# Edge values copied by products on GpSimd, and the filter's maxima begun twelve turns later, in a kernel of a spectral filter and a feed-forward block

## The chip, the cores and the metric

The kernel runs on one core of a Trainium2 chip. The metric is device time in microseconds (us) of one execution; the number given for a kernel is the median of its runs. The engines of the core are called by short names: PE (TensorE, matrix products), DVE (VectorE, elementwise work and reductions), ACT (ScalarE, activations and copies with a scale), POOL (GpSimd), SP (SyncE, which here only issues DMAs). Each works through its own list of instructions in order; semaphores make one wait for another.

## The reference

```python
def _layernorm(x, axis=-1, eps=1e-5):
    m = jnp.mean(x, axis=axis, keepdims=True)
    v = jnp.var(x, axis=axis, keepdims=True)
    return (x - m) / jnp.sqrt(v + eps)

xn = _layernorm(A_x)                         # (1, 2048, 1024)
X = jnp.fft.rfft2(xn, axes=(-2, -1))
s = jnp.fft.irfft2(X * (A_w_r + 1j * A_w_i), (2048, 1024), axes=(-2, -1))
h = _silu(jnp.einsum("bsd,df->bsf", xn, B_w1))      # w1: (1024, 3584)
g = _silu(jnp.einsum("bsf,fd->bsd", h, B_w2))       # w2: (3584, 1024)
return A_x + s * g
```

Two branches of the normalized input meet at the end: a filter in the frequency domain (a two-dimensional Fourier transform, a product with the complex weights `A_w_r`, `A_w_i`, and the inverse transform), and a feed-forward block with two weights.

## The kernel before

All large products run on PE in 16-bit numbers. Each 32-bit operand is scaled and split into a high and a low half (`high`, line 268, on ACT; `low`, line 271, on DVE), and each product is the sum of three. The scales are powers of two found from maxima: those of the first weight per pair of blocks, one for the whole second weight, and one for the filter's weights.

PE's work follows a fixed list, and the other engines' work is woven in while the program is built. Jobs are Python generators that lie in queues (`bg`, `wq`, `xq`, `yq`, `sq`). After each group of matmuls, `after` lets the finished PSUM tile be read out (`settle`) and gives one step to the first job in each queue (`work`); such a round is called a turn here. A job's step appends its instructions to the engines' lists at that place. So a job begun some turns later has its instructions some turns further down every list, and nothing else is moved except what waits for it to be done.

The stages, with their times in the trace:

- To 376 us: layer norm, and the first 16 of 28 blocks of the first product (`mm1`, line 620).
- 376 to 602 us: the other 12 blocks, made by seven products of half size instead of eight (`product`, line 658). There are 12 units of seven products, 84 turns, each of 12 matmuls; `plan` sets their order, in which the products of neighbouring units overlap. A unit has PSUM tiles `pa`, `pe` and `pc`. Products M1, M6, M7 and M4 add up in `pa`, and between them ACT copies it out: `pc<-pa` (line 670) after M1, `h<-pa` (672) after M6, 674 after M7, 678 after M4. So the next product of `pa` waits for that copy. DVE adds `pe` at lines 675 and 682. `hidden` (lines 710 to 713) then makes the seven sums of the hidden values, splits them (`hoone`, `hosum`) and stores them by POOL's queue (line 704).
- In the same stretch, three jobs prepare weights. `weights1` in `wq` loads the first weight's blocks (SP, line 406), takes maxima on ACT (290), reduces them over the partitions on POOL (417), computes scales on DVE (275 to 278), splits the blocks and combines their quarters (436 to 440) and splits those sums. `w2max_gen` in `xq` loads the second weight (SP, 476), takes its maxima on ACT and stores a difference (497, 499). `wmax_gen` in `yq` is the job that the change moves: 54 pieces of 128x304 of the filter's weights, each with a load by SP (1175) into one of three places and, two turns after, a reduction on DVE (1170); then one reduction over the 54 columns (1177), an all-reduce on POOL (1179), and five short steps on DVE for the scales `zs` and `s_sc` (241, 242, 1182 to 1184), which are used from 747 us on. It takes 60 steps, one a turn.
- The second weight's preparation, `w2_scales` (lines 241, 242, 521 to 526) and `w2_gen` (SP 558, splits 268 and 271), is begun when `w1j.done and not xq and not yq`, or at the first product of the last block pair (`q == NP - 1`, turn 68); there all steps that are left in `xq` and `yq` are made at once.
- 602 to 1261 us: the second product in seven parts (`mm2`, lines 786 to 788), with the filter woven in: forward transform (`fd_gen`), the transform along the sequence with the filter's weights (`f_gen`, from line 1235 on), the inverse (`i_chunk`). In `f_gen`, each of 16 tiles `X` gets a product with the weights, whose second part (1314) writes over `X`. In four of them the edge column is first saved to `xsv` by a copy on POOL (1296).

The job `wmax_gen` is begun where the job `t_job` is found done and `hold_x[0]` is still set, which is at turn 0: the first of its loads stands at 375.83 us, ahead of the first product.

Of the kernel before, what the change touches and what calls it, by code (L numbers as in the profile page):

```python
# [13 lines left out]
OP = mybir.AluOpType  # L14
# [34 lines left out]
def view(flat, off, shape, dtype):  # L49
    n = math.prod(shape[1:]) * (2 if dtype == F16 else 4)  # L50
    assert off % 4 == 0 and n % 4 == 0
    v = flat[:, off // 4:(off + n) // 4]
    if dtype != F32:
        v = v.bitcast(dtype)
    if len(shape) > 2:
        names = "abcdef"[:len(shape) - 1]
        v = v.rearrange(f"p ({' '.join(names)}) -> p {' '.join(names)}", **dict(zip(names, shape[1:])))
    return v
# [84 lines left out]
def spectral_ffn(ctx, tc, x, w_r, w_i, w1, w2, ca, kc, ci, tw, pm, out):  # L143
    nc = tc.nc
# [28 lines left out]
    def small(name, n=1):  # L173
        return sm.tile([128, n], F32, name=name)

    both = cp.tile([128, 256], F32, name="both")
    ident, ones = both[:, 0:128], both[:, 128:256]
    mhalf = small("mhalf")
    zp = cp.tile([128, 4, 4, 2, 2], F16, name="zp")
    xsv = cp.tile([128, 3, 4, 4, 2], F32, name="xsv")  # L180
    tws = cp.tile([128, 16], F32, name="tws")
# [58 lines left out]
    def pow2(e, m):  # L240
        nc.vector.tensor_single_scalar(e.bitcast(I32), m.bitcast(I32), 0x7F800000, op=OP.bitwise_and)
        nc.vector.tensor_single_scalar(e, e, 2.0**-100, op=OP.max)
# [922 lines left out]
    def wmax_gen():  # L1165

        mt, tl = small("mw", 54), {}
        for k in range(57):
            if k >= 3:
                nc.vector.tensor_reduce(mt[:, k - 3:k - 2], tl.pop(k - 3), axis=AX.X, op=OP.max, apply_absolute_value=True)  # L1170
            yield 0.5
            if k < 54:
                src = (w_r, w_i)[k // 27].rearrange("(p r) k -> p (r k)", p=128)
                tl[k] = view(R2[0], 72 * KB + 256 + 1216 * (k % 3), [128, 304], F32)
                nc.sync.dma_start(tl[k], src[:, 304 * (k % 27):304 * (k % 27 + 1)])
        m = small("mwx")
        nc.vector.tensor_reduce(m, mt, axis=AX.X, op=OP.max)
        mm = small("mwm")
        nc.gpsimd.partition_all_reduce(mm, m, 128, bass.bass_isa.ReduceOp.max)
        yield 0.3  # L1180
        pow2(e_w, mm)
        nc.vector.reciprocal(zs, e_w)
        nc.vector.tensor_single_scalar(zs, zs, 2.0**-26, op=OP.mult)
        nc.vector.tensor_single_scalar(s_sc, e_w, 2.0**-21, op=OP.mult)
        yield 0.3
# [15 lines left out]
    def part_of(u):  # L1201
        return u // 4, (u % 4 if u < 12 else (0, 1, 3, 2)[u % 4])
# [21 lines left out]
    def f_gen():  # L1224
# [57 lines left out]
        for u in range(16):  # L1282
            q, j = part_of(u)
# [9 lines left out]
            radix4(-1, b, d, X)  # L1293
            Xv = X.rearrange("m (a r) k -> m a r k", r=2)
            if j == 0:
                nc.gpsimd.tensor_copy(xsv[:, 0, q], Xv[:, :, :, 0])
            w_ = [B["w"][u // 2, i] for i in range(2)]
            for i in range(2 if u % 2 == 0 else 0):
                wf = w_[i].rearrange("m a k -> m (a k)")
# [347 lines left out]
    def finish(q, job):  # L1647
        while not job.done:
            slot(q)
# [34 lines left out]
    with tc.manual_schedule():  # L1684
# [3 lines left out]
        def add(q, gen):  # L1688
            j = Job(gen)
            q.append(j)  # L1690
            return j
# [14 lines left out]
        def after(ev):  # L1706
            settle()
            fresh_ev[0] = ev
            tick()
            work()  # L1710
# [14 lines left out]
        def spin(n):  # L1725

            if n:
                ps = pf.tile([128, 512], F32, name="spin", tag="ff")
                for _ in range(n):
                    nc.tensor.matmul(ps[:, 0:256], idle[:, 0:128], idle, start=True, stop=True)  # L1730
# [10 lines left out]
        slot(wq)  # L1741
        ln = [add(bg, ln_gen(0)), None, None, None]
        nc.gpsimd.memset(mhalf, -0.5)
        spin(WARM[0])
        for k, q in enumerate((bg, wq, bg, wq, bg, wq, bg, wq, wq)):
            slot(q)
# [61 lines left out]
        for n, (_, u, name) in enumerate(plan):  # L1808
            q, g = strassen[u]
            left = len(plan) - 1 - n  # L1810
            while q not in W:
                slot(wq)
            if not w2j and (w1j.done and not xq and not yq or q == NP - 1):
                finish(wq, w1j)
                while xq or yq:
                    slot(xq)
                    slot(yq)
                w2_scales()
                w2j = add(wq, w2_gen())
            if (q, g, name) == (NPL, 1, "M6"):  # L1820
                while not t_job.done:
                    slot(bg)
            if t_job.done and hold_x[0]:
                aux[:] = [Map({"x": [(X1, 0), (X1, 8 * KB)]}), 2]
                hold_x[0] = False
                add(yq, wmax_gen())
            ev = product(q, g, name)
            if (q, g, name) == (NP - 1, 0, "M3"):
                free0[0] = True
            if left == 6:  # L1830
                for j in range(3):
                    load_h(0, j, 0, nc.sync)
            after(ev)
            if not n:
                settle()
            if n < 8 or n % 7 in (1, 4) or w2j and left < 9:
                slot(wq)
# [98 lines left out]
```

## Time and profile before

| | us |
|---|---|
| runs | 1262.78, 1258.46, 1261.06; median 1261.06 |
| the profiled execution: its time | 1262.97 |
| its span, from the first instruction to the last | 1261.2 |
| mean granted clock of PE | 0.993 of full speed |
| PE busy in the span | 1233.3 |
| waits of PE, 0 to 376 us / 376 to 602 / 602 to 1261 | 12.4 / 5.8 / 3.0 |
| DVE's waits for the maxima's loads (line 1170) | 20.8 |

In the profile's rows, the first number of a line of time is the start in us, the second the duration; then engine, line of the kernel, operation, output and inputs by the program's names, and size. What stands in brackets is the idle time of the engine just before, and what ended it. A row that ends in x12 holds 12 instructions. Rows of waits read: who waited, for whom, us in total, times, longest. "SPq", "POOLq" and "ACTq" are instructions of an engine's queue that are not counted as busy time.

### The profile page before, as it was taken

The numbers are of one execution on the slowest core, as the hardware profiler recorded it, in microseconds if no ns is written. First come the engines' busy times: TensorE is split into PE (matmuls) and PEld (weight loads), VectorE is DVE, ScalarE is ACT, GpSimd is POOL, SyncE is SP. The second block draws the span as 40 slices with busy tenths as digits, with TensorE's granted clock in tenths as the row PEclk, the third lists the DMA queues.
The fourth block names the chain that finished last, engine by engine and source line by source line (L and its number), as shares of the span: only waits on it lengthen the run. The fifth ranks groups of instructions, "written<-read, shape, count | busy, mean of one in ns | idle before, by whom it ended". The sixth has DMA issues, their size and how long they took to land. (4 is left out here: it accounts for less than half of the span.)

```text
span 1261.2 us, 18558 instructions
## 1 busy us (share of the span) xinstructions
PE 1233.3 (98%) x6825; PEld 640.1 (51%) x6825; DVE 995.5 (79%) x1680; ACT 562.6 (45%) x827; POOL 264.8 (21%) x399
## 2 busy tenths in 40 slices
PE   7999999999999999999999999999999999999998
PEld 5544454444443444444545455555554455566654
DVE  5768989889996877887588949995999448977875
ACT  3676366655456867776423314222424222412221
POOL 1322343434242223143300000102112100110111
PEclk8999999999999999999999999999999999999999
DMA  8359687777468788867856798879989999987687
GB/s 285 109 101 249 164 286 224 221 216 208 119 170 248 232 272 246 253 198 253 305 166 188 250 227 299 283 209 292 274 289 266 366 319 309 313 282 272 222 271 269
DMA packets 174235, 306.68 MB, mean 243 GB/s; under 512 B 31808, under 2 KB 81984, under 8 KB 173120
## 3 DMA queue, kind: packets, MB, share of 16 engines
q1 hardware_dynamic: 127904, 162.80, 41.8%
q0 software_dynamic: 30448, 93.87, 25.9%
q10 hardware_dynamic: 15792, 48.83, 11.1%
q8 instruction: 53, 0.87, 0.3%
q14 instruction: 38, 0.31, 0.1%
HBM read 204.25 MB, written 111.67 MB: 250 GB/s over the span
## 5 line engine op out<-in xcount | busy, mean ns | idle before, releaser
L620 PE MATMUL pa<-xn,w 128*128 128x512 f16 x1536 | 333.6, 379 | 4.0 <-DVE w L271 1.9
L786 PE MATMUL pb<-r,w 128*128 128x512 f16 (+1 forms) x798 | 300.2, 376 | 2.7 <-DMA w<-hd_one 2.7
L788 PE MATMUL pb<-r,w 128*128 128x512 f16 (+1 forms) x798 | 300.2, 376 | 0.0
L787 PE MATMUL pb<-r,w 128*128 128x512 f16 (+1 forms) x798 | 300.0, 376 | 0.0
L620 PEld LDWEIGHTS <-w 128*128 128x128 f16 x1536 | 149.8, 98 | 183.5 <-DVE w L271 2.4
L658 PEld LDWEIGHTS <-w 128*128 128x128 f16 x1008 | 98.9, 98 | 127.0 <-issue 8.7
L788 PEld LDWEIGHTS <-w 128*128 128x128 f16 x798 | 78.3, 98 | 91.7 <-issue 0.8
L786 PEld LDWEIGHTS <-w 128*128 128x128 f16 x798 | 78.3, 98 | 88.9 <-DMA w<-hd_one 3.6
L787 PEld LDWEIGHTS <-w 128*128 128x128 f16 x798 | 78.3, 98 | 85.5 <-issue 0.8
L658 PE MATMUL pa<-r,w 128*128 128x512 f16 x432 | 100.8, 384 | 5.7 <-ACT h L672 3.5
L268 ACT ACTIVATE r<-r,sc 128x512 f16<-128x512 f32 x88 | 60.8, 715 | 90.7 <-DMA r<-in_B_w_dram 59.4
L704 POOL DMA_DIRECT2D hd_one<-hoone x54 | 51.0, 945 | 192.1 <-DVE hoone L271 150.4
L271 DVE SCALAR_TENSOR_TENSOR r<-r,sc 128x512 f16<-128x512 f32 x88 | 64.9, 748 | 25.4 <-ACT r L268 19.9
L271 DVE SCALAR_TENSOR_TENSOR hoone<-h,hs,hoone 128x2048 f16<-128x2048 f32 x28 | 65.7, 2346 | 7.1 <-ACT hoone L268 7.0
L268 ACT ACTIVATE hosum<-hr,hs 128x1536 f16<-128x1536 f32 x28 | 43.9, 1568 | 40.2 <-DVE hr L711 26.4
L271 DVE SCALAR_TENSOR_TENSOR hosum<-hr,hs,hosum 128x1536 f16<-128x1536 f32 x28 | 50.7, 1812 | 12.4 <-ACT hosum L268 12.4
L268 ACT ACTIVATE hoone<-h,hs 128x2048 f16<-128x2048 f32 x28 | 55.8, 1993 | 6.7 <-DVE h L713 3.9
L630 ACT ACTIVATE h<-pa,ep 128x512 f32<-128x512 f32 x64 | 42.8, 676 | 27.9 <-PE pa L620 27.6
L704 POOL DMA_DIRECT2D hd_sum_d<-hosum x26 | 23.0, 884 | 138.7 <-DVE hosum L271 96.1
L710 DVE TENSOR_TENSOR hr<-h 128x1024 f32<-128x1024 f32 x28 | 34.2, 1220 | 15.5 <-ACT h L630 14.0
L1512 PE MATMUL iu<-xn 128*128 128x256 f16 x384 | 44.6, 273 | 0.6 <-DVE xn L1564 0.3
L704 POOL DMA_DIRECT2D hd_sum<-hosum x52 | 44.7, 1034 | 0.0
(299 smaller groups left out, 2056.1 us busy)
## 6 DMA issues: line engine op xcount, KB each, us to landing
w<-hd_dif ACTq DMA_DIRECT2D x32, 448.0 KB, 6.1
r<-in_B_w_dram SPq DMA_DIRECT2D x56, 256.0 KB, 7.9
w<-hd_sum ACTq DMA_DIRECT2D x32, 448.0 KB, 7.0
w<-hd_one ACTq DMA_DIRECT2D x32, 448.0 KB, 6.3
hd_one<-hoone POOLq DMA_DIRECT2D x54, 256.0 KB, 4.9
hd_dif<-hoone POOLq DMA_DIRECT2D x54, 256.0 KB, 4.6
hd_sum<-hosum POOLq DMA_DIRECT2D x52, 256.0 KB, 5.9
xn<-in_B_w_dram SPq DMA_DIRECT2D x40, 256.0 KB, 4.6
```

What stands on the lines that cost most here:

```text
L268: nc.scalar.activation(hi, raw, AF.Copy, scale=scale)
L271: nc.vector.scalar_tensor_tensor(lo, raw, scale, hi, op0=OP.mult, op1=OP.subtract)
L620: nc.tensor.matmul(ps, w[:, wh, d], xt[:, xh, d], start=(n == 0), stop=(n == 23))
L630: nc.scalar.activation(hq[:, 2 * (c % 2) + f % 2], ps, AF.Silu, scale=ep[:, q:q + 1])
L658: nc.tensor.matmul(ps, lhs(d, wh), rhs(d, xh), start=(name in ("M1", "M5") and d + n == 0), stop=(d + n == 5), skip_group_check=True)
L704: defer(1, lambda k=k, m=m: stores[0].dma_start(hd[m, g][:, :, q].rearrange("f p h s -> f p (h s)"), o[:, k].rearrange("f p h s -> f p (h ...
L710: tt(sums[:, 0:2], hq[:, 0::2], hq[:, 1::2], op=OP.subtract)
L786: nc.tensor.matmul(ps, hh[:, 0], w[:, 0], start=first, stop=False)
L787: nc.tensor.matmul(ps, hh[:, 0], w[:, 1], start=False, stop=False)
L788: nc.tensor.matmul(ps, hh[:, 1], w[:, 0], start=False, stop=last)
L1512: nc.tensor.matmul(ps[:, q], lhs, rhs, start=(n == 0 and r == 0), stop=(n == 2 and r == 1))
```

## The change

Two edits. The four copies of edge values at line 1296 become products with a small tile of ones (`one8`, 8 columns, filled at the start by a memset on POOL). And the job of the filter's maxima is added to its queue at turn 12 of the seven-product part (`n == 12`), no longer where `hold_x[0]` falls; the two statements that stood before it stay there.

```diff
-    mhalf = small("mhalf")
+    mhalf, one8 = small("mhalf"), small("one8", 8)
...
             if j == 0:
-                nc.gpsimd.tensor_copy(xsv[:, 0, q], Xv[:, :, :, 0])
+                nc.gpsimd.tensor_tensor(xsv[:, 0, q], Xv[:, :, :, 0], one8.rearrange('m (a r) -> m a r', a=4), op=OP.mult)
...
         nc.gpsimd.memset(mhalf, -0.5)
+        nc.gpsimd.memset(one8, 1.0)
...
                 aux[:] = [Map({"x": [(X1, 0), (X1, 8 * KB)]}), 2]
                 hold_x[0] = False
+            if n == 12:
                 add(yq, wmax_gen())
```

PE's list is the same in both kernels. What moves stands on DVE, SP and POOL, and by a few rows on ACT. On DVE, at the tenth turn or so of the seven-product part, these rows stand before the change: the scale of a pair of blocks of the first weight (`ep`, `rs`, `hs`), the splits of two blocks (`w_67`) and the first of the combinations of quarters (in the staging buffer `r_2496`), with the filter's maxima (`mw`) between them.

```order
L1170 TENSOR_REDUCE mw<-r_2496 128x1
L275 TENSOR_SCALAR ep<-pm_223 128x1
L276 TENSOR_SCALAR ep<-ep 128x1
L277 RECIPROCAL rs_225<-ep 128x1
L278 TENSOR_SCALAR hs<-rs_225 128x1
L1170 TENSOR_REDUCE mw<-r_2496 128x1
L271 SCALAR_TENSOR_TENSOR w_67<-r_2496,rs_225,w_67 128x1024
L271 SCALAR_TENSOR_TENSOR w_67<-r_2496,rs_225,w_67 128x512
L436 TENSOR_TENSOR r_2496<-r_2496 128x512
L437 TENSOR_TENSOR r_2496<-r_2496 128x512
L1170 TENSOR_REDUCE mw<-r_2496 128x1
L439 TENSOR_TENSOR r_2496<-r_2496 128x512
```

The same place on DVE after the change:

```order
L275 TENSOR_SCALAR ep<-pm_224 128x1
L276 TENSOR_SCALAR ep<-ep 128x1
L277 RECIPROCAL rs_226<-ep 128x1
L278 TENSOR_SCALAR hs<-rs_226 128x1
L271 SCALAR_TENSOR_TENSOR w_67<-r_2498,rs_226,w_67 128x1024
L271 SCALAR_TENSOR_TENSOR w_67<-r_2498,rs_226,w_67 128x512
L436 TENSOR_TENSOR r_2498<-r_2498 128x512
L437 TENSOR_TENSOR r_2498<-r_2498 128x512
L439 TENSOR_TENSOR r_2498<-r_2498 128x512
```

The three reductions are gone from between them; so are the others of the first turns. The second place is on DVE at the last block pair, some 16 turns before the part ends. Before, the last scales of the second weight (`E1r`, `sc`, `c`) stand ahead of the sums of a unit's hidden values (`hr`, `h`) and of the addition of PE's tile `pe` (line 675), and behind it comes the first split of the second weight (`r_2496<-xn`).

```order
L523 RECIPROCAL E1r<-E_4785 128x1
L524 TENSOR_SCALAR sc_229<-ep,E1r 128x14
L525 TENSOR_SCALAR sc_229<-sc_229,r_4784 128x14
L526 TENSOR_SCALAR c_228<-e_4783,E_4785 128x1
L710 TENSOR_TENSOR hr_0_4807<-h_12_0_4640 128x1024
L711 TENSOR_TENSOR hr_0_4807<-h_12_0_4640 128x512
L713 TENSOR_TENSOR h_12_0_4640<-h_12_0_4640 128x2x512
L675 TENSOR_TENSOR h_12_1_4780<-h_12_1_4780,pe_1_4692 128x512
L271 SCALAR_TENSOR_TENSOR r_2496<-xn,sc_229,r_2496 128x512
```

After the change there stand, from the row before the same addition (line 675) on, the last maxima, the reduction over their columns (`mwx`), the filter's scales (`e_w`, `zs`, `s_sc`) and the first row of the second weight's scales (`e_4815`):

```order
L1170 TENSOR_REDUCE mw<-r_2498 128x1
L675 TENSOR_TENSOR h_12_1_4767<-h_12_1_4767,pe_1_4671 128x512
L1170 TENSOR_REDUCE mw<-r_2498 128x1 x2
L1177 TENSOR_REDUCE mwx<-mw 128x1
L241 TENSOR_SCALAR e_w<-mwm 128x1
L242 TENSOR_SCALAR e_w<-e_w 128x1
L1182 RECIPROCAL zs<-e_w 128x1
L1183 TENSOR_SCALAR zs<-zs 128x1
L1184 TENSOR_SCALAR s_sc<-e_w 128x1
L241 TENSOR_SCALAR e_4815<-w2s 128x1
```

The second weight's scales have moved from ahead of line 675 to behind the filter's scales, which wait for POOL's all-reduce (`mwm`); 8 more reductions of the maxima stand above, between the scale of the last pair of blocks and line 710, and one between lines 713 and 675. On ACT the first three splits of the second weight now stand together behind line 678 and ahead of line 672. On SP, the last nine loads of the maxima stand one behind the other, with no load of another job between them, and the loads of the second weight's pieces (line 558) follow them. The third place is POOL at the edge values, behind the stores of the forward transform (`vd`). Before:

```order
L1120 DMA vd_82<-xn 512x1x512
L1120 DMA vd_83<-r_2496 512x1x512
L1296 COPY xsv<-xn 128x8 x2
L563 DMA r_2496<-in_B_w_dram 128x512
L1258 DMA zd<-xn 128x4096
```

After:

```order
L1120 DMA vd_82<-xn 512x1x512
L1120 DMA vd_83<-r_2498 512x1x512
L1296 ISA
L1296 TENSOR_TENSOR xsv<-xn,one_215 128x8 x2
L563 DMA r_2498<-in_B_w_dram 128x512
L1258 DMA zd<-xn 128x4096
```

The row `ISA` is new; it waits for nothing of its own, and the first product behind it waits for DVE, as the copy did.

## The prediction

> **What bounds the kernel now.** I read the page's busy times first, then the waits of TensorE (PE), then PE's line of time through the seven-product part, and then, for each wait there, the engine that released it, in its own line of time.
>
> ```profile
> PE 1233.3 (98%) x6825; PEld 640.1 (51%) x6825; DVE 995.5 (79%) x1680; ACT 562.6 (45%) x827; POOL 264.8 (21%) x399
> ```
>
> PE is busy for 1233.3 of 1261.2 us, and the change takes no product away from it and moves none. All that it can win is PE's idle time, and all that it can lose is new idle time there. The list of PE's waits (waiting tile and line, whom it waited for: us in total, times, longest):
>
> ```profile
> PE tp L956 <- ACT x L947: 7.5, 1, 7.5
> ...
> PE pa L658 <- ACT h L672: 3.5, 4, 2.4
> ...
> PE pa L658 <- ACT pc L670: 2.3, 2, 1.5
> ```
>
> The first stands at the start of the kernel. The other two lie in the seven-product part (376 to 602 us), where the filter's maxima run. PE's line of time there, with its idle time in brackets, shows them one by one; after 537.38 PE waits for nobody until that part ends:
>
> ```profile
> 405.54 4.44 PE L658 MATMUL pa<-r,w 128*128 128x512 f16 x12 [2.38 <-ACT h L672]
> ...
> 480.30 2.75 PE L658 MATMUL pa<-r,w 128*128 128x512 f16 x12 [0.40 <-ACT h L672]
> ...
> 494.93 2.75 PE L658 MATMUL pa<-r,w 128*128 128x512 f16 x12 [1.52 <-ACT pc L670]
> ...
> 518.58 2.75 PE L658 MATMUL pa<-r,w 128*128 128x512 f16 x12 [0.18 <-ACT h L672]
> ...
> 537.38 2.75 PE L658 MATMUL pa<-r,w 128*128 128x512 f16 x12 [0.51 <-ACT h L672]
> ```
>
> That is 2.38 + 0.40 + 1.52 + 0.18 + 0.51 = 4.99 us on which moving the maxima can act: 0.4% of the time. VectorE (DVE) is busy 79% of the span and is not the bound; it matters only where ScalarE (ACT), waiting for DVE, reads a PSUM tile too late for PE.
>
> **The maxima, at their old place.** They are 54 loads on SyncE's queue (SP) and 54 reductions on DVE, at the latter's line:
>
> ```profile
> L1170 DVE TENSOR_REDUCE mw<-r x54: 459/463/472, 387.3 to 537.3; 128x1 f32<-128x304 f32 x54
> ```
>
> Begun twelve turns later, loads and reductions leave the stretch before some 411 us. (A turn is one product of 12 matmuls. Where PE does not wait, three take 573.64 - 565.87 = 7.77 us by two rows below, 2.59 each. The product of 405.54 is turn 10, counted from 0, so turn 12 starts at 410.7.) Of PE's waits only the one of 2.38 us lies in that stretch. It follows back through ACT and DVE so (DVE first, then ACT):
>
> ```profile
> 394.19 0.46 DVE L1170 TENSOR_REDUCE mw<-r 128x1 f32<-128x304 f32 x1
> ...
> 396.31 1.95 DVE L271 SCALAR_TENSOR_TENSOR w<-r,rs,w 128x1024 f16<-128x1024 f32 x2 [0.65 <-ACT w L268]
> ...
> 399.63 0.46 DVE L1170 TENSOR_REDUCE mw<-r 128x1 f32<-128x304 f32 x1
> 400.01 0.68 DVE L439 TENSOR_TENSOR r<-r 128x512 f32<-128x512 f32 x1
> ```
>
> ```profile
> 395.13 1.76 ACT L268 ACTIVATE w<-r,rs 128x1024 f16<-128x1024 f32 x2 [1.90 <-DVE rs L277]
> ...
> 401.45 2.19 ACT L268 ACTIVATE w<-r,rs 128x1024 f16<-128x1024 f32 x2 [2.86 <-DVE r L440]
> ...
> 404.91 0.58 ACT L672 ACTIVATE h<-pa 128x512 f32<-128x512 f32 x1
> ```
>
> PE waits for ACT's copy at 404.91 (L672). It stands behind the weight split of 401.45, which waited 2.86 us for DVE's L440, the last of four combinations of weights; these stand behind the split on DVE at 396.31, which waited for ACT's split of 395.13, which waited for DVE's scale (L277). Two reductions stand inside that chain, at 394.19 ahead of the scale and at 399.63 between the combinations. Each holds DVE for 0.38 us (399.63 to 400.01, the next start). A third one falls into the 0.65 us in which DVE waited for ACT anyway, and counts nothing. So L440, the split and L672 come 2 x 0.38 = 0.76 us earlier, and PE's wait falls from 2.38 to 1.62 us: **-0.76 us**. The rest stays because ACT's own row of work and the scale remain. The other four waits, 2.61 us, lie after 411 us, where DVE and SP have the same rows in the same order as before (every turn still has one load and one reduction, and twelve turns later the same ones of another number). I leave them as they are.
>
> **The maxima, at their new end.** Now they end at 565 instead of 538 us, beside the last turns. Here PE did not wait, so the change can only cost, and the question is how much cover there is. The rows of DVE there (in `e_w` L241 to L1184 the filter's scale, at 557.71 the scales of the second weight, at 561.95 the sum that reads PE's tile `pe`), of PE, of POOL and of ACT:
>
> ```profile
> 541.69 0.14 DVE L241 TENSOR_SCALAR e_w<-mwm 128x1 int32<-128x1 int32 x1
> ...
> 542.38 1.22 DVE L710 TENSOR_TENSOR hr<-h 128x1024 f32<-128x1024 f32 x1
> ...
> 557.71 0.15 DVE L241 TENSOR_SCALAR e<-w2s 128x1 int32<-128x1 int32 x1
> ...
> 559.08 1.21 DVE L710 TENSOR_TENSOR hr<-h 128x1024 f32<-128x1024 f32 x1
> ...
> 561.95 0.68 DVE L675 TENSOR_TENSOR h<-h,pe 128x512 f32<-128x512 f32 x1
> ...
> 564.15 2.35 DVE L271 SCALAR_TENSOR_TENSOR hoone<-h,hs,hoone 128x2048 f16<-128x2048 f32 x1 [0.86 <-ACT hoone L268]
> ```
>
> ```profile
> 565.87 2.75 PE L658 MATMUL pe<-xn,w 128*128 128x512 f16 x12
> ...
> 573.64 2.75 PE L658 MATMUL pa<-r,w 128*128 128x512 f16 x12
> ```
>
> ```profile
> 540.91 0.42 POOL L1179 PARTITION_ALL_REDUCE mwm<-mwx  x1
> ...
> 550.91 2.38 POOL L514 PARTITION_ALL_REDUCE w2s<-w2x  x1 [9.57 <-DVE w2x L513]
> ```
>
> ```profile
> 590.49 1.32 ACT L268 ACTIVATE r<-xn,sc 128x512 f16<-128x512 f32 x2
> ```
>
> Between the scale at 541.69 and L675, DVE gets 9 more reductions (3.42 us), and loses the filter's scale (542.38 - 541.69 = 0.69) and the second weight's (559.08 - 557.71 = 1.37), which come later: +1.36 us. L675 then ends at 561.95 + 1.36 + 0.68 = 563.99, and PE writes `pe` again at 565.87: 1.88 us are left, so no wait. Behind L675 come two more reductions (to 564.75), the last one over the 54 columns (0.15, as the short step at 541.69), and POOL's all-reduce, for which DVE now has to stand: between 0.42 and 2.38 us by the two rows. POOL's queue holds nothing else then, which speaks for the small end; both are kept. Queued behind that wait on DVE are the two scales and the low halves of the hidden values, for which only POOL's stores wait. With the two scales (2.06) the second weight's is ready between 567.4 and 569.3. Waiting for it: three splits on ACT (0.66 each by the pair at 590.49, 2.0 in all) and behind them L672 (0.58), which PE's product of 573.64 needs: done between 570.0 and 571.9. That is 1.7 us or more before PE asks. **0 us**, with a narrow cover; what breaks it is a rival below.
>
> **The copies of edge values.** Four copies on POOL, each of 128x8, become products with a tile of ones. The profile has no product of this shape; its bounds are the copy at 750.51 and the longest product on POOL, of 128x1:
>
> ```profile
> 0.87 0.10 POOL L1743 MEMSET mhalf<- 128x1 f32 x1
> 12.73 0.18 POOL L944 TENSOR_SCALAR v<-mv 128x1 f32<-128x1 f32 x1 [11.77 <-issue]
> ...
> 68.61 1.25 POOL L372 PARTITION_ALL_REDUCE pm<-m  x1 [5.86 <-issue]
> 79.18 0.19 POOL L944 TENSOR_SCALAR v<-mv 128x1 f32<-128x1 f32 x1 [9.31 <-DVE mv L942]
> ...
> 84.46 2.00 POOL L945 TENSOR_TENSOR v<-v,mhalf 128x1 f32<-128x1 f32 x1
> ```
>
> ```profile
> 734.07 0.71 POOL L1120 DMA_DIRECT2D vd<-r  x1 [3.98 <-DVE r L1116]
> 750.51 0.19 POOL L1296 COPY xsv<-xn 128x8 f32<-128x8 f32 x1 [15.74 <-DVE xn L258]
> ```
>
> ```profile
> 747.82 0.69 DVE L1290 TENSOR_TENSOR xn<-fx,xn 128x512 f32<-128x512 f32 x1 [7.17 <-ACT xn L1255]
> ...
> 751.99 1.23 DVE L1314 TENSOR_TENSOR xn<-xn 128x1024 f32<-128x1024 f32 x1 [0.20 <-DVE xn L1313]
> ```
>
> So 0.19 to 2.00 us; I take 0.5, nearer to the copy, since 8 columns are hardly more work than one. The tile is written over by DVE at L1314, 1.48 us after the copy starts; only a product above that holds DVE, by 0.5 us at most, four times, and PE has not waited for DVE in that stretch even where DVE itself stood for 7.17 us. 0 us. The new memset follows the one at 0.87 and puts back POOL's first work, at 12.73, for which ACT and then PE (7.5 us, above) wait: as long as a memset, **+0.10 us**, and 0 to 0.15.
>
> The built order also has a new instruction on POOL ahead of the first product. In the trace such rows stand where POOL changes between all-reduces and arithmetic, as configurations:
>
> ```profile
> L372 POOLq MODIFY_POOL_CONFIG  x4: 11/202/394, 62.9 to 141.5; - x4
> ```
>
> ```profile
> L944 POOLq MODIFY_POOL_CONFIG  x4: 11/47/83, 1.0 to 69.9; - x4
> ```
>
> After the configuration at 62.9 the all-reduce starts at 68.61 and after that at 1.0 the first arithmetic starts at 12.73: 5.7 and 11.7 us, in which POOL waited for nothing shown. After the one at 69.9 the arithmetic starts at 79.18, when its input comes, and waits no longer: 9.3 us covered it. Here the new one follows the store of 734.07, and waits for nothing; the input comes at 750.51, 15.7 us later. It is covered: 0 us.
>
> **The sum.** -0.76 + 0.10 = -0.66 us. On the profiled execution's own 1262.97 us (1261.2 of span) that is 1262.31; this execution was 0.15% above the median of the runs, so on the median of 1261.06 it is **1260.4 us**. A measurement of this kernel can tell about 0.3%, 3.8 us, from no change.
>
> **The rivals.** *No gain:* what is won at 405 us is given back at 480 or 495, if those waits hang on transfers that do not come earlier with PE. For it speaks that 0.76 is less than the 1.52 there; against it that SP's loads are themselves released by DVE's and ACT's work. 1261.06 + 0.10 = 1261.2.
>
> *Faster:* all five waits go, because SP, freed at the start, has the other weights' loads ahead of ACT for the whole part. 1261.06 - 4.99 + 0.10 = 1256.2. Against it: the four later waits lie where SP has its old rows.
>
> *Slower, by late loads at the new end.* The trace's loads of the maxima take, from issue to landing:
>
> ```profile
> DMA to landing us min/median/max: 2.2/4.8/11.5
> ```
>
> The 54th load follows the 51st reduction, which by the sums above (8 more reductions, less 2.06) ends at 559.08 + 0.98 = 560.1. With 4.8 us it lands at 564.9, just after DVE wants it; with 11.5 at 571.6. Then the scale is ready 0.38 + 0.15 + 0.42 to 2.38 + 2.06 us later, L672 is done at 577.2 to 579.2, and PE stands from 573.64: 3.6 to 5.6 us, 1264.0 to 1266.0. It decides from a landing time of 6 to 8 us. For it speaks that POOL's stores of hidden values are under way then; against it that SP has no load of another kind between the last nine there, while before it had.
>
> *Slower, by the configuration.* If the 5.7 to 11.7 us came only once the product is ready, it would start at 756.2 to 762.2 and hold DVE's L1314 by 4.2 to 10.2 us; less the 7.17 that DVE stood without harm to PE, 0 to 3.0 us: 1260.4 to 1263.4. Against it speaks the row at 79.18. [...]
>
> **How the numbers follow.** The forecast gets 0.57, no gain 0.15, faster 0.08, late loads 0.14, the configuration 0.06. Faster by over 0.3% (below 1257.3): half of the faster case and a little of the measurement's own spread, 0.06. Slower by over 0.3% (above 1264.8): half of the late loads and a fifth of the configuration, and a little spread, 0.10. The same: 0.84. The range takes in half of either outer case: 1257.2 to 1264.6.
>
> **What would show it.** In the profile after, PE's wait for L672 near 405 us should be about 1.6 us, its waits between 480 and 540 as before, and none between 550 and 600; the configuration should stand near 735 us, and the products of L1296 be under 1 us with no wait of L1314 for POOL. A wait of PE behind L672 or L675 near 566 or 574, or of DVE for the maxima's last loads of more than 2 us, would prove the cover at the new end too narrow. A gap between the configuration and the first product that reaches beyond 751 would prove the configuration uncovered. I am wrong if the time leaves 1257 to 1265, or if PE's waits in the seven-product part change by more than 2 us.

## The result and the profile after

The changed kernel takes 1256.14 us (median of 20 runs, 1251.67 to 1259.94); the kernel before takes 1262.49 (20 runs) beside it. The ratio is 0.9948, with a 95% interval of 0.9934 to 0.9961: faster by half a per cent. The forecast was 0.05% and the time lies below the range. The profiled execution took 1256.27 us and has a span of 1254.5, 6.7 us less than before's.

Three boundaries of the two traces say where they went. (The first product of the first layer, L620, opens the matrix work; the first of L658 the seven-product part; the first of L786 the second layer.)

| | before, us | after, us | difference |
|---|---|---|---|
| first L620 | 25.79 | 19.00 | -6.8 |
| first L658 | 376.2 | 369.5 | -6.7 |
| length of the seven-product part, first L658 to first L786 | 225.9 | 224.3 | -1.7 |
| from there to the end of the span | 659.1 | 660.8 | +1.7 |

So nearly the whole gain is made in the first 19 us, where the prediction had +0.10. PE's busy time, from the page of the profile after, fell too:

```profile
PE 1229.1 (98%) x6825; PEld 637.1 (51%) x6825; DVE 995.0 (79%) x1680; ACT 563.1 (45%) x827; POOL 264.8 (21%) x400
```

It was 1233.3 us for the same 6825 matmuls: 4.2 of the 6.7 us are busy time and only the rest is idle time, so some matmuls ran faster. (1.2 of the 4.2 lie in the idle work at PE's very start, L1730, ahead of all that is looked at here: 35 matmuls in 6.77 us before and 5.58 after. The kernel before with a late product, below, has 6.79 there, so this share is not shown to be the change's.) PE's waits after the change (waiting tile and line, whom it waited for: us in total, times, longest):

```profile
PE tp L956 <- ACT x L947: 3.2, 3, 2.4
PE pa L658 <- ACT h L672: 3.1, 3, 1.8
...
PE pa L658 <- ACT pc L670: 1.6, 2, 1.4
PE fx L1235 <- DMA r<-in_B_w_dram: 1.3, 1, 1.3
```

The first row was 7.5, once. Followed back on POOL, in its line of time after the change:

```profile
0.90 0.11 POOL L1744 MEMSET one<- 128x8 f32 x1
6.38 0.19 POOL L944 TENSOR_SCALAR v<-mv 128x1 f32<-128x1 f32 x1 [5.38 <-DVE mv L942]
```

POOL's first arithmetic stands at 6.38 us, right behind its input, which DVE finishes at 6.08 + 0.21 = 6.29. Before it stood at 12.73, although the same input was there at 5.96 + 0.21 = 6.17, as DVE's line of time before the change has it:

```profile
5.96 0.21 DVE L942 BATCH_NORM_AGGREGATE mv<-st 128x2 f32<-128x12 f32 x1
```

PE follows: its first work behind the wait for ACT (L956) moves from 15.29 to 8.96 us, by 6.33, and the first L620 by 6.8. The clock is a likely part of the difference. In the kernel before the granted clock is 0.50 from 10.1 to 20.4 us, part of it under work of PE, as this stretch of the kernel before shows (busy times by engine, PE first; the third number from the end is the granted clock); after the change no stretch before 20 us has a dropped clock.

```profile
16.00:18.00 2.00, 2.00 (x11) 2.00 (x11) 0.00 (x0) 1.21 (x2) 1.42 (x5) 0.50 0.50 183
```

The new memset is there (0.11 us at 0.90), in front of that work, and costs nothing, since the input comes at 6.29. What is gone is the stretch of idle time behind the configuration of POOL at 1 us, 11.7 us long before. Such a stretch, from a configuration to the first work that could start, is called POOL's load here; the trace shows its length and not what fills it. The configuration itself still stands there. The groups of POOL's queue after the change, by line; the last row is the new one, ahead of the products:

```profile
L372 POOLq MODIFY_POOL_CONFIG  x4: 6/202/397, 55.9 to 134.8; - x4
```

```profile
L944 POOLq MODIFY_POOL_CONFIG  x4: 11/47/83, 1.2 to 63.1; - x4
```

```profile
L1296 POOL TENSOR_TENSOR xsv<-xn,one x4: 199/963/1783, 742.1 to 922.3; 128x8 f32<-128x8 f32 x4
L1296 POOLq MODIFY_POOL_CONFIG  x2: 108/108/108, 726.9 to 726.9; - x2
```

Read as a list in time, POOL is configured in turn for arithmetic (L944) and for the all-reduce (L372). Before, the last of all stands at 141.5 us, for the all-reduce. After, it stands at 726.9, for arithmetic. That gave the theory to test.

**Theory R.** My supposition is that POOL holds one of two loaded programs, and keeps it from one execution to the next; the traces show configurations and times alone. By it the arithmetic at the start waits for a load only where the execution before left the all-reduce's program there. The products change which one is left, and so pay off at the start of the next execution. **Rival M:** the moved maxima bring the gain. **Rival S:** it is the start's own list with the memset of ones, or the products themselves.

In the seven-product part the wait near 405 us changed as follows in PE's line of time after:

```profile
372.95 2.76 PE L658 MATMUL pa<-r,w 128*128 128x512 f16 x12 [0.73 <-DMA wt<-in_B_w_dram]
398.19 2.75 PE L658 MATMUL pa<-r,w 128*128 128x512 f16 x12 [1.76 <-ACT h L672]
471.90 2.75 PE L658 MATMUL pa<-r,w 128*128 128x512 f16 x12 [0.81 <-ACT h L672]
486.44 2.75 PE L658 MATMUL pa<-r,w 128*128 128x512 f16 x12 [1.43 <-ACT pc L670]
523.09 2.75 PE L658 MATMUL pa<-r,w 128*128 128x512 f16 x12 [0.16 <-ACT pc L670]
528.99 2.75 PE L658 MATMUL pa<-r,w 128*128 128x512 f16 x12 [0.56 <-ACT h L672]
```

The wait is 1.76 and was 2.38. But look at the second number of that row: the twelve products take 2.75 us, where the row of before, which the prediction quotes, has 4.44. That is another 1.69 us. **Theory K:** the idle time of 2.38 us is long enough for PE's granted clock to drop, 1.76 is not. The stretches of the kernel before around it:

```profile
403.10:405.50 2.40, 0.06 (x1) 0.00 (x0) 2.40 (x4) 2.37 (x7) 0.00 (x0) 1.00 1.10 245
405.50:406.50 1.00, 0.96 (x4) 0.44 (x4) 0.59 (x1) 1.00 (x2) 0.00 (x0) 0.78 1.09 260
406.50:407.50 1.00, 1.00 (x3) 0.29 (x2) 0.00 (x0) 0.42 (x3) 0.00 (x0) 0.50 1.07 327
407.50:408.50 1.00, 1.00 (x4) 0.37 (x3) 0.16 (x1) 0.51 (x2) 0.00 (x0) 0.50 1.19 352
408.50:409.50 1.00, 1.00 (x4) 0.36 (x3) 1.00 (x2) 0.00 (x0) 0.00 (x0) 0.51 1.14 300
409.50:410.50 1.00, 1.00 (x6) 0.43 (x5) 1.00 (x3) 0.49 (x1) 0.00 (x0) 1.00 1.11 297
```

The clock falls to 0.50 at 406 us and is back at 409.5: some 3.4 us at half speed, which cost 1.7. Its rival is that the products are slowed by what runs beside them, the reductions and their loads.

### The profile page after: what moved, and what is told of

Read it like the earlier page. It is cut to its first block, busy times and chain, and to the rows that moved or that the text cites. A ratio compares the mean times of both kernels' runs of the same rounds, so it can differ in the third digit from the quotient of the medians.

```text
span 1254.5 us, 18566 instructions
## 1 busy us (share of the span) xinstructions
PE 1229.1 (98%) x6825; PEld 637.1 (51%) x6825; DVE 995.0 (79%) x1680; ACT 563.1 (45%) x827; POOL 264.8 (21%) x400
## 5 line engine op out<-in xcount | busy, mean ns | idle before, releaser
L620 PE MATMUL pa<-xn,w 128*128 128x512 f16 x1536 | 333.7, 379 | 4.2 <-DVE w L271 1.9
L786 PE MATMUL pb<-r,w 128*128 128x512 f16 (+1 forms) x798 | 300.2, 376 | 2.7 <-DMA w<-hd_one 2.7
L620 PEld LDWEIGHTS <-w 128*128 128x128 f16 x1536 | 149.8, 98 | 183.7 <-DVE w L271 2.4
L658 PEld LDWEIGHTS <-w 128*128 128x128 f16 x1008 | 98.6, 98 | 125.7 <-issue 6.7
L786 PEld LDWEIGHTS <-w 128*128 128x128 f16 x798 | 78.2, 98 | 89.1 <-DMA w<-hd_one 3.6
L658 PE MATMUL pa<-r,w 128*128 128x512 f16 x432 | 99.1, 379 | 5.5 <-ACT h L672 3.1
L271 DVE SCALAR_TENSOR_TENSOR hosum<-hr,hs,hosum 128x1536 f16<-128x1536 f32 x28 | 50.7, 1812 | 12.7 <-ACT hosum L268 12.7
L1235 PE MATMUL fx<-xn 128*128 128x256 f16 x192 | 43.2, 272 | 2.0 <-DMA r<-in_B_w_dram 1.3
```

The lines of the kernel that those rows point to most:

```text
L271: nc.vector.scalar_tensor_tensor(lo, raw, scale, hi, op0=OP.mult, op1=OP.subtract)
L620: nc.tensor.matmul(ps, w[:, wh, d], xt[:, xh, d], start=(n == 0), stop=(n == 23))
L658: nc.tensor.matmul(ps, lhs(d, wh), rhs(d, xh), start=(name in ("M1", "M5") and d + n == 0), stop=(d + n == 5), skip_group_check=True)
L786: nc.tensor.matmul(ps, hh[:, 0], w[:, 0], start=first, stop=False)
L1235: nc.tensor.matmul(o, k[:, c, kh, 1], v[:, c, vh], start=(n == 0), stop=False)
```

## The experiments

All were timed against the kernel before in the same sessions, in five rounds each (6 to 12 runs of each kernel); its median there was 1262.2 to 1263.6, so ratios compare better than times. The table gives for each what POOL is last configured for, the start of its first arithmetic (L944) and of PE's first L620, the seven-product part's length, all from its profile, and then the time.

| kernel | POOL's last configuration | L944 | first L620 | part | median | ratio to before (95%) |
|---|---|---|---|---|---|---|
| before | all-reduce | 12.73 | 25.79 | 225.9 | 1262.49 | 1 |
| after | arithmetic | 6.38 | 19.00 | 224.3 | 1256.14 | 0.9948 (0.9934 to 0.9961) |
| products alone | arithmetic | 6.39 | 18.77 | 225.9 | 1257.05 | 0.9953 (0.9937 to 0.9969) |
| maxima alone | all-reduce | 11.35 | 24.67 | 223.8 | 1262.30 | 0.9990 (0.9978 to 1.0002) |
| before + late product | arithmetic | 6.55 | 18.80 | 226.0 | 1255.98 | 0.9945 (0.9930 to 0.9960) |
| after + late all-reduce | all-reduce | 10.67 | 23.72 | 223.3 | 1261.69 | 0.9992 (0.9978 to 1.0006) |
| memset alone | all-reduce | 12.16 | 25.21 | 225.3 | 1262.77 | 0.9997 (0.9984 to 1.0010) |
| after + late all-reduce + late product | arithmetic | 6.12 | 18.57 | 223.2 | 1256.67 | 0.9953 (0.9935 to 0.9970) |
| after + all-reduce at the edge values | arithmetic | 6.15 | 18.8 | 223.2 | 1260.76 | 0.9986 (0.9970 to 1.0001) |

**Either edit alone.** The products with their memset, and the maxima's line alone:

```diff
             if j == 0:
-                nc.gpsimd.tensor_copy(xsv[:, 0, q], Xv[:, :, :, 0])
+                nc.gpsimd.tensor_tensor(xsv[:, 0, q], Xv[:, :, :, 0], one8.rearrange('m (a r) -> m a r', a=4), op=OP.mult)
...
+        nc.gpsimd.memset(one8, 1.0)
```

> The products and the memset of ones alone; the maxima stay where the kernel before has them. Theory R (an execution starts with the GpSimd program that the execution before it configured last; the products leave the arithmetic one there, so the load at the start goes): GpSimd's first arithmetic (L944) near 6.4 us and not 12.7, the first mm1 matmul near 19.0 and not 25.8, and 6.8 us less in all, less what the change in whole gained in the seven-product part: about 1256.5 by device time, a ratio of 0.9948 to 0.9960. Rival M (the moved maxima brought the gain): the start as before, a ratio of 1.000.

```diff
+            if n == 12:
                 add(yq, wmax_gen())
```

> The moved maxima alone; copies as before, no ones. Theory R: the last configuration stays the all-reduce's, so L944 near 12.7 us and the first mm1 near 25.8 as before; in the seven-product part the longest wait for L672 goes from 2.4 to 1.8 us; in all 0 to 1.6 us less, a ratio of 0.9987 to 1.000. Rival M: the start near 19.0 and a ratio of 0.995.

The products alone give 0.9953 and the start of the changed kernel. In POOL's line of time with the products alone:

```profile
6.39 0.19 POOL L944 TENSOR_SCALAR v<-mv 128x1 f32<-128x1 f32 x1 [5.38 <-DVE mv L942]
```

The maxima alone leave the start late (L944 at 11.35) and give 0.9990, within what can be told from no change. Rival M falls. In the seven-product part it is the other way round: the products alone leave it at 225.9 us, the maxima alone shorten it to 223.8. That is too little for the times to show: 0.9990 is not told from 1, nor 0.9948 from 0.9953.

**The last configuration, without the edits.** Into the kernel before, one useless product of 128x1 in the inverse transform (`i_chunk`, near 1010 us), where POOL stands idle:

```diff
                 nc.gpsimd.tensor_copy(C["z"][c][:, :, :, :, 0, 0], zp[:, c])
+                if c == IORDER[0]:
+                    nc.gpsimd.tensor_tensor(small("late2"), e_w, e_w, op=OP.mult)
```

> The kernel before with its copies and maxima, and one product of 128x1 on GpSimd, of no use to the result, put into the gradient's part at a place (about 1010 us) where GpSimd stands idle. Theory R: this leaves the arithmetic program configured last, so the start goes as after the change: L944 near 6.4 us, first mm1 near 19.0, 6.5 us less in all, a ratio near 0.995; the load near 1010 us is covered. Rival S (the memset of ones, or the products themselves, brought the gain): start as before, a ratio of 1.000 or a little over.

(The expectations call this place the gradient's part; there is no gradient here, it is the inverse transform.) Nothing of the change is in this kernel, and nothing ahead of 1010 us differs from before. Its POOL line of time:

```profile
6.55 0.19 POOL L944 TENSOR_SCALAR v<-mv 128x1 f32<-128x1 f32 x1 [5.58 <-DVE mv L942]
...
1018.54 0.18 POOL L1590 TENSOR_TENSOR late<-e_w 128x1 f32<-128x1 f32 x1 [7.28 <-issue]
```

A product at 1018 us has moved the work at 12.7 us to 6.55. Nothing that stands late in a program can act on its own start; it acts on the next execution's. The ratio is 0.9945, all that the change won. Rival S falls with it: there is no memset here, and the copies are as before.

**The last configuration, against the edits.** Into the changed kernel, at the same place, one useless all-reduce:

```diff
+                if c == IORDER[0]:
+                    nc.gpsimd.partition_all_reduce(small("late"), e_w, 128, bass.bass_isa.ReduceOp.max)
```

> The changed kernel with one all-reduce of 128x1, of no use to the result, put into the gradient's part near 1010 us, so that the all-reduce program is configured last. Theory R: the start's load comes back: L944 near 12.7 us, first mm1 near 25.8, 6.5 us more than the changed kernel, so 0 to 1.6 us less than before, a ratio of 0.9987 to 1.000. Rivals M and S (maxima, the start's own list): both edits are in, so the ratio stays near 0.995 and the first mm1 near 19.0.

```profile
10.67 0.18 POOL L944 TENSOR_SCALAR v<-mv 128x1 f32<-128x1 f32 x1 [9.66 <-DVE mv L942]
...
1018.62 0.38 POOL L1590 PARTITION_ALL_REDUCE late<-e_w  x1 [6.16 <-issue]
```

The start is late again, by 4.3 us rather than 6.35, since the load took less here, and the gain is gone: 0.9992, with products, ones and moved maxima all in place. (The releaser named in the row is only the last semaphore: that `mv` was done at 5.80 + 0.21.)

**Both late instructions**, the all-reduce and then the product:

> The changed kernel with both late instructions near 1010 us: the all-reduce and then a product, neither of use to the result. Theory R: what counts is the last configuration alone, which is the arithmetic one again: L944 near 6.4 us, first mm1 near 19.0, a ratio near 0.995. Rival (an all-reduce late in the program, or the work there, costs the start or the end by itself): a ratio of 0.9987 to 1.000 as with the all-reduce alone.

```profile
6.12 0.19 POOL L944 TENSOR_SCALAR v<-mv 128x1 f32<-128x1 f32 x1 [5.12 <-DVE mv L942]
...
1012.61 0.38 POOL L1590 PARTITION_ALL_REDUCE late<-e_w  x1 [6.25 <-issue]
1023.15 0.18 POOL L1592 TENSOR_TENSOR late<-e_w 128x1 f32<-128x1 f32 x1 [10.16 <-issue]
```

The gain is back, 0.9953. So the late all-reduce costs nothing by itself: what counts is which configuration is the last.

**The memset alone** (`one8` and its memset in the kernel before):

> The kernel before with the tile of ones and its memset at the start, and nothing else. Theory R: the start's load stays, L944 near 12.7 us, the first mm1 at 25.8 to 25.95, 0 to 0.15 us more: a ratio of 0.9995 to 1.0005. Rival S (the start's own list brought the gain): first mm1 near 19.0, a ratio of 0.995.

0.9997, L944 at 12.16: as theory R had it.

**The load, uncovered.** In the changed kernel, an all-reduce of one column between the arrival of the first edge values and their product:

```diff
+                if u == 0:
+                    nc.gpsimd.partition_all_reduce(small("late"), X[:, 0, 0:1], 128, bass.bass_isa.ReduceOp.max)
                 nc.gpsimd.tensor_tensor(xsv[:, 0, q], Xv[:, :, :, 0], one8.rearrange('m (a r) -> m a r', a=4), op=OP.mult)
```

> The changed kernel with an all-reduce of 128x1, of no use to the result, between the arrival of the first filter step's values and its first product, so that both loads stand there uncovered. Theory R: the last configuration is still the arithmetic one, so the start stays near 19.0; VectorE's L1314 then waits for GpSimd 12 to 24 us once (two loads of 5.7 to 11.7 us each and the reduction), and TensorE waits for it less what the products ahead of it cover: 1256.1 plus 0 to 20 us. If the loads show no time in the middle of a program (rival: only a start pays), the wait for GpSimd at L1314 stays under 6 us and the time near 1256 to 1260.

POOL's line of time, and then DVE's:

```profile
739.83 0.45 POOL L1297 PARTITION_ALL_REDUCE late<-xn  x1 [15.81 <-DVE xn L255]
749.52 0.20 POOL L1298 TENSOR_TENSOR xsv<-xn,one 128x8 f32<-128x8 f32 x1 [9.25 <-issue]
```

```profile
749.76 1.23 DVE L1316 TENSOR_TENSOR xn<-xn 128x1024 f32<-128x1024 f32 x1 [7.71 <-POOL xsv L1298]
```

I had counted two loads and there is one. The all-reduce starts at 739.83, when its input comes; POOL's last configuration ahead of it was the all-reduce's, at 134.5 us, so by theory R no load was due. The one in front of the product takes 9.25 us and holds DVE for 7.71 (L1316 in this kernel is the line that is L1314 in the others). In the changed kernel the configuration stands at 726.9 and the product starts at 742.15, behind its input, and L1314 waits 0.2 us for it. The kernel takes 1260.76 us, 4.6 more than the changed one, and the intervals of the two ratios do not meet. Whether those 4.6 us come from the load is not settled. PE waits for nobody from 592 us, the end of the seven-product part, to 898; then it stands for 5.2 us, by the profile for DVE's L1347, and the clock is at 0.50 from 901.4 to 908.3. This stretch holds the loss: from the part's end to the end of the span the profile has 665.2 us against 660.8. But DVE is at the same place at 875 us in both kernels again, and PE waits 3.3 us there with the products alone, where no load was added. In front of an all-reduce POOL's idle time behind the configuration is 5.6 us (the kernel before with the late product) to 6.3 (both late instructions), in front of the arithmetic 7.3 to 11.7.

**The clock: a wait made longer, and the same work beside it.** Three useless activations of 128x1 in the changed kernel, directly ahead of the L672 that ends PE's wait, and then the same three one turn later (`n == 10`), behind it:

```diff
+            if n == 9:
+                for _ in range(3):
+                    nc.scalar.activation(small("late"), mhalf, AF.Copy)
             ev = product(q, g, name)
```

> The changed kernel, with three activations of 128x1 on ScalarE, of no use to the result, directly ahead of the L672 for which TensorE waits 1.76 us: that L672 and the wait end about 0.6 us later (three by about 0.2), so TensorE idles about 2.4 us, as before the change. Theory K: the granted clock drops to 0.50 for 3.4 us behind it and the twelve products take about 4.4 us and not 2.75; the seven-product part 2.3 us longer than the changed kernel's 224.2 (0.6 of wait, 1.7 of slow products), the time 1258.4, a ratio to before near 0.9965. Rival (only the wait counts): 0.6 us longer, 2.75 us for the twelve, a ratio near 0.995. The start stays near 19.0 by both.

> The same three activations in the changed kernel, but directly behind that L672 and its L683, where TensorE's longest wait is already over. By theory K and by its rival alike: the wait stays near 1.76 us, the twelve products take 2.75 us, the seven-product part 224.2 us (0 to 0.6 more), a ratio to before near 0.995. If the three activations by themselves slowed the products, the twelve would take over 4 us here too.

PE's line of time with the three ahead:

```profile
399.52 4.36 PE L658 MATMUL pa<-r,w 128*128 128x512 f16 x12 [2.31 <-ACT h L672]
```

and with the three behind:

```profile
398.02 2.75 PE L658 MATMUL pa<-r,w 128*128 128x512 f16 x12 [1.76 <-ACT h L672]
```

In the first, the granted clock has the stretch at half again:

```profile
399.50:400.50 1.00, 0.98 (x5) 0.48 (x5) 0.39 (x1) 1.00 (x2) 0.00 (x0) 1.00 1.11 320
400.50:401.50 1.00, 1.00 (x4) 0.30 (x2) 1.00 (x2) 0.91 (x4) 0.00 (x0) 0.50 0.81 154
```

0.66 us of work on ScalarE lengthened the wait by 0.55 and the twelve products by 1.61. The same work one place further down did neither. The part is 225.6 us with the three ahead and 224.0 with them behind: 1.3 more than the changed kernel's and not the 2.3 expected, since the waits further on are shorter by 0.6. The times are 1257.98 (0.9963, 0.9950 to 0.9976) and 1256.08 (0.9955, 0.9939 to 0.9972): 1.9 apart, where 2.3 was expected, and the intervals overlap. The traces decide this, for theory K.

**The clock: a wait filled.** In the kernel before, matmuls whose result nobody reads, in front of the twelve products; first ten of 128x256 by `spin(10)`, then four of 128x512:

```diff
+            if n == 10:
+                ps = pf.tile([128, 512], F32, name="spin", tag="ff")
+                for _ in range(4):
+                    nc.tensor.matmul(ps, idle[:, 0:128], xnT[2 * g][:, 0, 0], start=True, stop=True)
             ev = product(q, g, name)
```

> The kernel before, with ten more matmuls on ones (128x256, their result is never read) queued on TensorE in front of the twelve products that wait 2.38 us for ScalarE's L672. They run inside that wait and shorten its idle part by about 1.1 us; the list of every other engine is the same, the maxima stay at their old place. Theory K (after an idle time as long as 2.38 us the granted clock drops to 0.50 for 3.4 us, and the following matmuls lose 1.7 us; at 1.75 us it didn't): the twelve products take 2.75 us and not 4.44, the granted clock stays 1.00, the seven-product part lasts 224.2 us and not 225.9, in all 1.7 us less, a ratio of 0.9987. Rival (the slow products come from what runs beside them, the reductions or the loads): they stay at 4.44 us, the part at 225.9 or a little over, a ratio of 1.000 to 1.001. The start stays as before by both (L944 at 10.7 to 12.7 us).

> The kernel before, with four matmuls of 128x512 on values that are there already (their result is never read) queued on TensorE in front of the twelve products that wait 2.38 us for ScalarE's L672: about 0.9 us of work (4 by 0.22) inside that wait. Theory K (the long idle time drops the granted clock to 0.50 for 3.4 us): the twelve products take 2.75 us and not 4.44, no stretch at 0.50 behind them; the seven-product part gets 0.8 to 1.7 us shorter than before's 225.9, as far as the four don't wait for a PSUM buffer themselves. Rival (the slow products come from what stands beside them): 4.44 stays. The start as before by both.

(The first of the two no longer computes the reference's result, and no run shows why. The order of PE's list is not touched by that.) PE's lines of time, first with ten and then with four:

```profile
403.63 1.27 PE L1730 MATMUL spin<-both 128*128 128x256 f16 x10 [1.91 <-ACT both L290]
404.73 2.75 PE L658 MATMUL pa<-r,w 128*128 128x512 f16 x12
```

```profile
403.62 1.04 PE L1830 MATMUL spin<-xn,both 128*128 128x512 f16 x4 [1.90 <-ACT both L290]
404.49 2.75 PE L658 MATMUL pa<-r,w 128*128 128x512 f16 x12
...
493.02 4.44 PE L658 MATMUL pa<-r,w 128*128 128x512 f16 x12 [2.09 <-ACT pc L670]
```

The twelve products take 2.75 us with the maxima still beside them, so it is the idle time and not the company: theory K. But the time did not follow: 0.9996 (0.9976 to 1.0016) and 1.0005 (0.9991 to 1.0018). The added matmuls waited 1.9 us themselves. The row names ScalarE's L290 and the tile `both`: the maxima of L290 write a by-product over `both`, and the added matmuls read a half of that same tile. So the values were not "there already", as the second expectation had it, and PE's list is late; the part is 225.2 and 226.2 us. And in the second kernel the drop came back at 493, behind a wait of 2.09 us that is 1.52 in the kernel before.

**The same at another wait.** In the changed kernel, eight such matmuls in front of two steps of the second layer at which PE waits near 1000 us:

```diff
+            if n in (76, 77):
+                spin(8)
             mm2(m, j, banks[m, j], k, qs=range(4))
```

> The changed kernel, with eight such matmuls in front of each of the two steps of the second layer (the 77th and the 78th) at which TensorE waited 1.3 to 4.1 us in the profiles so far. Theory K: where the wait there is long enough to drop the clock (a drop at 1004 us in the changed kernel's profile, 1.7 us), the matmuls hold it up: no stretch at 0.50 near 1000 to 1010 us, and 0 to 1.7 us less than the changed kernel, a ratio to before of 0.993 to 0.995. Rival (they come too late or last over the end of the wait): 0 to 1.7 us more than the changed kernel, a ratio of 0.995 to 0.9965.

```profile
1006.00 1.86 PE L1730 MATMUL spin<-both 128*128 128x256 f16 x8 [4.13 <-DVE pl L835]
```

Those of the second step waited 4.13 us for a PSUM buffer that DVE had not yet read, and ran at the dropped clock (1.86 us for eight, 1.04 in front of the first step); it stays at 0.50 for 6.8 us, where the changed kernel has 3.4 us near 1004. The time is 1259.67 us (0.9962, 0.9943 to 0.9982), by the medians 3.5 more than the changed kernel, though the intervals overlap. The trace speaks for the rival here, and this is no way to a faster kernel. Nothing that I ran beats the changed kernel by more than can be told; the kernel before with its late product (1255.98) equals it.

## Why the prediction was wrong

**What failed** is above all one step: "The new memset follows the one at 0.87 and puts back POOL's first work, at 12.73, for which ACT and then PE (7.5 us, above) wait: as long as a memset, +0.10 us". It took the 11.7 us behind the configuration at 1.0 us for a fixed price of every execution. By the runs above they depend on what the execution before configured last on POOL (L944 at 12.73 us with the all-reduce, at 6.55 with a late product), and the change alters that. The products, whose configuration the prediction priced at 0 us, are what alters it. The term was -6.8 us (first L620 25.79 to 19.00) in place of +0.10; the products with their memset do the same without the maxima, a useless product at 1018 us does it without any edit, and an all-reduce at 1018 undoes it.

The rows to see it were quoted. After the configurations at 62.9 and at 1.0 the prediction counted 5.7 and 11.7 us of load; it asked where the *new* configuration would be paid, found it covered, and stopped. It did not ask why an execution has to load arithmetic at 1.0 at all, before POOL has done anything else. The answer, that the last configuration of the list was the all-reduce's, at 141.5, stood in the row of L372 itself.

**The maxima at the old place**: right in its mechanism and too small. The wait fell by 0.62 us (2.38 to 1.76; predicted 0.76). The term that was missed stands in the very row that the prediction took the wait from: twelve products in 4.44 us, with 2.75 in each of the four other rows. The drop of the clock was worth 1.69 us more. It counts as busy time, so the opening, "All that it can win is PE's idle time", was wrong as well. The five kernels of the table with the moved maxima have a part of 223.2 to 224.3 us, the four without 225.3 to 226.0.

The other waits came out close to what was said, but not one by one. Those of 0.40, 1.52 and 0.51 became 0.81, 1.43 and 0.56; the one of 0.18 went, and one of 0.16 came at another place (523.09). The first differs among the kernels with the maxima at their old place too (0.40 to 1.09), so its growth is not shown to come from the change. And the prediction's list left out a sixth wait, which also lies ahead of 411 us; the change left it at 0.73. The row of before:

```profile
379.68 2.76 PE L658 MATMUL pa<-r,w 128*128 128x512 f16 x12 [0.73 <-ACT pc L670]
```

All waits of the part together went from 5.72 to 5.45 us, so most of what the part gained is the clock's.

**The maxima at the new end**: right. PE waits for nobody from 529 us to the end of the part. DVE's line of time there:

```profile
554.85 0.67 DVE L675 TENSOR_TENSOR h<-h,pe 128x512 f32<-128x512 f32 x1
555.44 0.46 DVE L1170 TENSOR_REDUCE mw<-r 128x1 f32<-128x304 f32 x1
556.24 0.47 DVE L1170 TENSOR_REDUCE mw<-r 128x1 f32<-128x304 f32 x1 [0.34 <-DMA r<-in_A_w_i_dram]
556.74 0.21 DVE L1177 TENSOR_REDUCE mwx<-mw 128x1 f32<-128x54 f32 x1
557.43 0.15 DVE L241 TENSOR_SCALAR e_w<-mwm 128x1 int32<-128x1 int32 x1 [0.48 <-POOL mwm L1179]
```

The last load was 0.34 us late and the all-reduce cost 0.48 of waiting, the small end of what was allowed. The rival of late loads did not come.

**The products**: 0.20 to 1.78 us each, as bounded, though two of the four took over 1 us, and L1314 waited 0.2 us, once, as before. The prediction quoted the shortest of the copies; all four have the same spread as the products:

```profile
L1296 POOL COPY xsv<-xn x4: 190/419/1786, 750.5 to 928.1; 128x8 f32<-128x8 f32 x4
```

Their configuration was covered: at 726.9, the product at 742.15. The rival of the uncovered configuration was rightly set aside. The kernel that makes it true is 4.6 us slower, where I had 0 to 3.0, but the way from the load to PE is open.

**The rival "faster"** named 1256.2 us, which is what was measured, by a mechanism that did not happen: all five waits, 4.99 us, were to go, and 5.45 us of waits (the sixth included) are still there in that part. A total that agrees shows nothing of its cause.

**The rest**: +1.7 us from the part's end to the end of the span, on which the prediction said nothing. In the profile PE's waits there went from 3.0 to 4.7 us, 1.3 of it for a load at 901 us. These waits differ from profile to profile: at that place 3.3 us with the products alone, 0.5 with both late instructions, none in the kernel before; in all 4.4 with the memset alone, in which nothing stands at that place that the kernel before doesn't have. The 3.0 of the kernel before is the least of all profiles, so the +1.7 is not shown to come from the change.

## What to carry to other kernels

Where a trace shows configurations of an engine with idle time behind them, as POOL's here, write down their order as a ring: in this kernel what stood last in one execution decided whether the first arithmetic of the next started at 6.1 to 6.6 us or at 10.7 to 12.7. The change altered which kind of work is the last, and that was worth 6.8 us by the start of L620, though the last configuration stands at 726.9 us; one useless instruction at 1018 us showed it. And when a wait is to be shortened, read how fast the work behind it runs: near 405 us the price of the wait was 2.38 us of idle time and 1.69 us of slower products behind it.

## What the hardware did that I had not expected

- POOL's last configuration acts on the next execution. In the eight kernels whose last configuration is the arithmetic one L944 stands at 6.1 to 6.6 us and the first L620 at 18.5 to 19.8; in the six with the all-reduce's last, at 10.7 to 12.7 and 23.7 to 25.8. That it is the loaded program that stays is inferred from this; the trace shows only the times.
- The load in front of the arithmetic had no fixed length: 7.3, 9.25, 10.2 and, at the start, 9.7 to 11.7 us. The one in front of the all-reduce took 5.6 to 6.3.
- An idle time of PE of 2.31 to 2.39 us in the seven-product part was followed by the clock at 0.50 every time (five profiles), one of 1.75 to 1.91 at the same place never (nine profiles). A drop in that part lasted some 3.4 us (406.1 to 409.5 in the kernel before) and cost some 1.7 (4.44 us against 2.75). It is not a matter of length alone: at the start of the changed kernel PE idles for 2.39 us with no drop, and at 493 us 2.09 sufficed. In the six kernels with the late start the clock is at 0.50 for 6.8 to 10.2 us there, and of the eight others in one, that with the uncovered load, for 3.4. The ends of that range are two and three times 3.4; no run shows what sets the length of a drop.
